# Attention and two MLPs on one core: from the eleventh head on, `v` in two float16 parts and four products a tile instead of three parts and five

## The chip, the cores and the metric

The kernel runs on one core of a Trainium2 chip. The metric is the device time of one execution in microseconds (us), lower is better. Three runs of the kernel before are given, and one further execution that was profiled.

## The reference

```python
scores = scale * np.matmul(q, k.transpose(0, 1, 3, 2))          # 4 batches, 8 heads, 576 positions, 64 wide
decay = cum[:, :, :, None] - cum[:, :, None, :]                 # cum: cumulative sum of log f
scores = np.where(causal, -1000000000.0, scores + decay)
attn = np.exp(scores - np.max(scores, axis=-1, keepdims=True))
attn = attn / (np.sum(attn, axis=-1, keepdims=True) + 1e-09)
x = np.matmul(attn, v)                                          # then (2304, 512)
h = x @ w_in                                                    # 512 -> 2048
x = (np.maximum(h, 0.0) + alpha * np.minimum(h, 0.0)) @ w_out   # 2048 -> 512
out = ((x @ w_a) * (x @ w_b)) @ w_o                             # 512 -> 1536 -> 512
```

All is float32, so the kernel makes its products from parts: a float32 value is a high part plus a remainder, and a product is the sum of the products of the parts that matter.

## The kernel before

**Order of the work.** 32 heads (4 batches of 8) are worked off one after another in `attention()`. Step u runs a list of short operation names that is written out by hand (`_P["even"]`, `_P["odd"]`; `even0` and `odd0` for u below 10): `s0` to `s3` make the scores of head u in four blocks of 128 rows (128, 256, 384 and 512 columns wide) and their softmax numerators, `R` those of the last 64 rows of two heads, `h*` and `l*` split the numerators of head u-1 into two float16 parts and send them through a transposing DMA, `p0` to `p2` multiply the transposed parts of head u-2 with `v` (`pv`), `ri` and `rr` make the reciprocals of the row sums, `T` and `Q` prepare and load `q` and `k`, `V` loads `v` of head u+2, `vs` splits `v` of head u, `X` transposes the result of two heads. Each `M` hands over to the first MLP: from step 10 on `mlp1a` fills the places between with matmuls of the first seven of 16 blocks of `w_in` and `w_out` (names `h`, `y`), for half a batch (288 tokens) at a time. A scheduler then puts the instructions of each engine in an order of its own, within the dependences. After the heads come the rest of the first MLP (`hb`, `ya`) and the second one (`p`, `o`), with no part in the change.

**`v` before.** `load_v` (L344) brings a head into one of five buffers `vs` of three planes, 5 tiles of 128x64 each; the fifth tile has only 64 real rows. `split_v` (L351) makes two remainders on GpSimd, each by a subtraction of 128x320 (L357), so that the high halves of the three planes are three bfloat16 parts. Of the first ten heads six are kept `whole` (heads 0, 1, 4, 5, 8 and 9), with float32 products; all others take this split.

**The products.** `pv` (L511) has 15 tiles a head (10 below the diagonal and on it, 5 for the last rows), and of each five products with 64 columns:

```python
ph, pl = PT[m, grp][:, 2 * b], PT[m, grp][:, 2 * b + 1]
parts = [(ph, 0), (ph, 1), (ph, 2), (pl, 0), (pl, 1)]
for x, (p, i) in enumerate(parts):
    pe.matmul(o, p, high(vs[:, i, t]), start=start and x == 0, stop=stop and x == len(parts) - 1)
```

The numerators carry a factor 2^15 (`PSCALE`); `rinv` (L425) takes it out together with the row sum.

**Queues around it.** All loads and transposes are issued by the sync engine (SP) in order. GpSimd also makes the remainder of the MLP's activations, `g` (L651), which follows `lu` (ScalarE, L648), `lt` (VectorE, L649) and the cast of `g` (ScalarE, L650), and which the `y` matmuls need (L655). At the start GpSimd runs one chain of memsets (`ap_["pool"]`) for the constants of the attention, and behind it those of `rows`, from which the sync engine stores the decay sums.

Of the kernel before, what the change touches and what calls it, by code (L numbers as in the profile page):

```python
# [29 lines left out]
TB = 384  # L30
NQ = 5
PSCALE = 2.0 ** 15
MASK = -8.0e9


REBIAS = 2.0 ** -112
_P = dict(
    even="T h3 h2 h0 h1 s2 vs M Q s0 M l3 l2 s3 ri M p1 s1 l1 l0 M p0 p2 V M W".split(),
    odd="h3 h2 h0 h1 R vs M Q l3 l2 T s2 M h4 s3 ri M p1 s1 l1 l0 M p0 p2 rr s0 V W l4 M X".split(),
    split=0,  # L40
    lag=2,
    eng={'hi': 'act', 'lo': 'act', 'r': 'pool'},
# [7 lines left out]
    es=10,  # L50
    eng0={'e0': 'act', 'e2': 'act', 'e3': 'dve', 'e4': 'act'},
    even0='s3 T p1 s2 vs s0 Q M M M M h3 h2 h0 h1 l1 l2 p0 s1 l0 l3 ri p2 V W M'.split(),
    odd0='h3 h2 h0 h1 R M Q l2 T l3 M p1 s3 h4 s2 l1 l0 M M s1 s0 ri rr p0 vs p2 V W l4 M X'.split(),
)
PSM = _P["psm"]
LAG = _P["lag"]
# [4 lines left out]
def whole(n):  # L61

    return n < NATIVE and n // 2 % 2 == 0
# [26 lines left out]
def decay_attention_then_two_mlps(ctx, tc, q, k, v, f, w_in, w_out, alpha, w_a, w_b, w_o, out):  # L90
# [178 lines left out]
    def attention_setup():  # L269
        a = lpool(right, "att1", 1, "right")  # L270
        ap_["a"] = a
        maskz = a.tile([128, ST + 128 + S - HB], BF16, name="maskz")
        with tc.issue_after(ap_["pool"]):
            pool.memset(maskz, 0.0)
        tri = maskz[:, ST:ST + 128]
        ap_["pool"] = pool.affine_select(
            out=tri, in_=tri, pattern=[[-1, 128]], compare_op=ALU.is_ge, fill=MASK, base=0, channel_multiplier=1,
        ).ins

        def zeros(x):  # L280
            with tc.issue_after(ap_["pool"]):
                ap_["pool"] = pool.memset(x, 0.0).ins
        rest = maskz[:, ST + 128:]
        for j in range(2):
            act.copy(rest[64 * j:64 * j + 64, S - HB - SR:], tri[0:64, 0:SR])
        ap_["mask"] = maskz
        ap_["mask_r"] = rest

        for i in range(2):
            z = ST + SR * (1 - i)  # L290
            scores_set(a, i)
            rq = a.tile([64, SP], F32, tag=f"RQ_{i}", name=f"RQ_{i}")
# [12 lines left out]
        for nm in ("nmr", "smr"):
            ap_[nm] = a.tile([128, 2], F32, tag=nm, name=nm)
        for i in range(5):

            ap_["vs", i] = a.tile([128, 3, NQ, D], F32, tag=f"vs_{i}", name=f"vs_{i}")
            zeros(ap_["vs", i][SR:, :, 4])  # L310

    def load_qk_pool():
        ident = ap_["ident"] = lpool(right, "ident", 1, "right").tile([128, 128], F32, name="ident")
# [31 lines left out]
    def load_v(n):  # L345
# [2 lines left out]
        sp.dma_start(vs[:, 0, 0:4], v[b, h, 0:ST].rearrange("(p t) d -> p t d", p=128))  # L348
        sp.dma_start(vs[0:SR, 0, 4], v[b, h, ST:])

    def split_v(n):  # L351

        if whole(n):
            return
        vs = ap_["vs", n % 5]
        for i in range(2):
            pool.tensor_tensor(vs[:, i + 1], vs[:, i], high(vs[:, i]), op=ALU.subtract)  # L357

# [33 lines left out]

    def scores(n, i):
        w = 128 * (i + 1)
        o = bank(f"sc_{n}_{i}")[:, 0:w]
        products(o, n, 128 * i, 0, w, True, True)
        return o

    def softmax_in(n, i, o):
        s = s_view(n, i)  # L400
        m = ap_["mask"][:, ST - 128 * i:ST - 128 * i + 128 * (i + 1)]
        nm, sm = (ap_[x, n % 2][:, i:i + 1] for x in ("nm", "sm"))
        dve.tensor_tensor_reduce(s, o, m, -0.125, 3.0e38, ALU.add, ALU.min, nm)  # L403
        act.activation(s, s, AF.Exp, bias=nm, scale=-1.0, accum_out=sm)  # L404

    def scores_rest(n):
# [15 lines left out]
        dve.tensor_tensor(nm[:, 0:1], nm[:, 0:1], nm[:, 1:2], op=ALU.min)  # L422
        act.activation(s[:, :S], s[:, :S], AF.Exp, bias=nm[:, 0:1], scale=-1.0, accum_out=sm[:, 0:1])

    def rinv(n, sm, ri):  # L425
        dve.tensor_scalar(sm, sm, 1e-9, 1.0 if whole(n) else PSCALE, op0=ALU.add, op1=ALU.mult)
        dve.reciprocal(ri, sm)

    PT = {}
# [84 lines left out]
    def pv(u, c):  # L514

        g, j = divmod(u, 2)
        vs = ap_["vs", u % 5]
        if u not in ps_x:
            pl = "mm" if u + LAG < max(_P["first"], NATIVE) else "at"
            ps_x[u] = ps[pl].tile([128, 512], F32, tag=pl, name=f"pv_{u}")  # L520
        ps_o = ps_x[u]

        def products(o, m, grp, b, t, start, stop):
            if whole(u):
                pe.matmul(o, P32[m, grp][:, b], vs[:, 0, t], start=start, stop=stop)
                return
            ph, pl = PT[m, grp][:, 2 * b], PT[m, grp][:, 2 * b + 1]
            parts = [(ph, 0), (ph, 1), (ph, 2), (pl, 0), (pl, 1)]
            for x, (p, i) in enumerate(parts):
                pe.matmul(o, p, high(vs[:, i, t]), start=start and x == 0, stop=stop and x == len(parts) - 1)  # L530

        if c < 2:
            for i in (2 * c, 2 * c + 1):
                for t in range(i + 1):
                    products(ps_o[:, D * i:D * i + D], u, GROUP[i], FIRST[i] + t, t, t == 0, t == i)
            return
        for t in range(NQ):
# [48 lines left out]
    def attention():  # L586

        cur = lambda u: 0 <= u < NI
        if LAG == 2:
            load_v(0)  # L590
            load_v(1)
        warm_up(_P.get("wu", [0, 0])[0], "a")
        stack(0)
        warm_up(_P.get("wu", [0, 0])[1], "b")
        load_qk(2)
        if NATIVE > 3:
            load_qk(3)
        yield "W", -1
        for u in range(NI + LAG):
            ap_["u"] = u  # L600
            for op in order(u):
                a, i = op[0], op[-1]
                if op in ("M", "W"):
                    yield op, u
                elif op == "ri":
                    if cur(u - 1):
                        rinv(u - 1, ap_["sm", (u - 1) % 2], ap_["ri", (u - 1) % 2])
                elif op in ("h4", "l4"):
                    m = u if u % 2 else u - 1
                    if cur(m):  # L610
                        (p_hi if a == "h" else p_lo)(m, 4)
                elif a in "hl":
                    if cur(u - 1):
                        (p_hi if a == "h" else p_lo)(u - 1, int(i))
                elif op == "R":
                    if cur(u):
                        softmax_rest(scores_rest(u))
                elif op == "rr":
                    if cur(u):
                        rinv(u, ap_["smr"][:, 0:1], ap_["rir", u // 2 % 2])  # L620
                elif a == "s":
                    if cur(u):
                        softmax_in(u, int(i), scores(u, int(i)))
                elif op == "T":
                    if cur(u + 1):
                        stack(u + 1)
                elif op == "Q":
                    if u > 1 and cur(u + 2):
                        load_qk(u + 2)
                elif op == "V":  # L630
                    if cur(u + 4 - LAG):
                        load_v(u + 4 - LAG)
                elif op == "vs":
                    if cur(u + 2 - LAG):
                        split_v(u + 2 - LAG)
                elif op in ("p0", "p1", "p2"):
                    if cur(u - LAG):
                        pv(u - LAG, int(i))
                elif op == "X":
                    if cur(u - 3):  # L640
                        turn((u - 3) // 2)
# [448 lines left out]
```

## Time and profile before

| | us |
|---|---|
| median of 3 runs | 1050.09 |
| lowest, highest | 1049.08, 1052.24 |
| the profiled execution | 1054.88 |
| its span in the trace | 1053.1 |

The span is the time from the first to the last instruction of the program on the core; the profiled execution has 1.8 us around it. Its own time is 4.79 us above the median. PE is the matmul engine, DVE is VectorE, ACT ScalarE, POOL GpSimd, SP the sync engine, whose issues have the letter q behind the name. An instruction's record reaches from its start to its end; on PE, ACT and DVE the next one can start before that.

### The profile page before, as it was taken

To read this page: it belongs to the slowest core of one execution; us is meant where nothing else is said; L and a number is where in the kernel's file an instruction comes from. 1 tells how busy PE (TensorE), PEld (TensorE's weight loads), DVE (VectorE), ACT (ScalarE), POOL (GpSimd) and SP (SyncE) were. 2 spreads that over 40 slices of the span, in tenths; PEclk is the share of its full clock that TensorE was granted. 3 is DMA by queue.
4 is the path that set the end of the run, shared out by engine and by line. 5 is a ranking of instruction groups with operands and counts; after the bars stand their busy time and mean duration, and the time that the engine had idled before them with its cause. 6 is when DMAs were issued, how large, how long until landed. Compare 5 with 4: busy or idle time off the path is not lost.

```text
span 1053.1 us, 20143 instructions
## 1 busy us (share of the span) xinstructions
PE 1008.3 (96%) x7485; PEld 955.5 (91%) x7485; DVE 704.1 (67%) x1455; ACT 460.2 (44%) x1041; POOL 412.5 (39%) x415
## 2 busy tenths in 40 slices
PE   4788999999999999999999998999999999999998
PEld 3677999999999999999999997999989999899997
DVE  5899878878866275443557749665985558965553
ACT  4767777777865354333344343222442123321110
POOL 4424423324232255333456677322543224531111
PEclk9899999999999999999999999999999999999999
DMA  6995779987994758556668995835338384453623
GB/s 168 211 204 128 192 154 155 218 170 158 225 152 78 250 163 256 195 190 192 228 215 275 345 366 199 319 104 216 110 101 310 114 307 135 124 207 124 250 90 111
DMA packets 191783, 202.90 MB, mean 193 GB/s; under 512 B 99460, under 2 KB 160388, under 8 KB 191684
## 3 DMA queue, kind: packets, MB, share of 16 engines
q1 hardware_dynamic: 191684, 201.60, 65.7%
q8 instruction: 59, 0.97, 0.4%
q14 instruction: 40, 0.33, 0.1%
HBM read 130.07 MB, written 50.17 MB: 171 GB/s over the span
## 4 chain that ended last, share of the span: by engine, by line
PE 75%; DVE 11%; DMA 5%; issue 3%; POOL 3%; ACT 1%; SPq 1%; POOLq 0%; DVEq 0%; ACTq 0%
PE p L654 7%; PE p L656 7%; PE p L655 7%; PE pv L530 5%; PE o L654 4%; PE o L655 4%; PE o L656 4%; PE ya L654 3%; PE ya L655 3%; PE ya L656 3%; PE hb L654 3%; PE hb L656 3%; PE hb L655 3%; PE h L654 2%; PE y L655 2%
## 5 line engine op out<-in xcount | busy, mean ns | idle before, releaser
L654 PE MATMUL p<-yq,w_h 128*128 128x384 f32 x360 | 121.7, 338 | 2.3 <-DVE lu L1033 1.4
L656 PE MATMUL p<-yq,w_h 128*128 128x384 f32 x360 | 121.3, 337 | 0.0
L655 PE MATMUL p<-yq,w_h 128*128 128x384 f32 x360 | 121.1, 336 | 0.0
L654 PE MATMUL o<-w_o,gg 128*128 128x512 f32 x216 | 84.7, 393 | 1.7 <-ACT gg L1014 1.7
L404 ACT ACTIVATE s<-s,nm 128x512 f32<-128x512 f32 (+3 forms) x128 | 71.5, 560 | 32.9 <-DVE nm L403 31.9
L655 PE MATMUL o<-w_o,gg 128*128 128x512 f32 x216 | 84.9, 393 | 0.0
L357 POOL TENSOR_TENSOR vs<-vs 128x320 f32<-128x320 f32 x52 | 43.4, 835 | 101.9 <-DMA vs<-in_v 96.7
L656 PE MATMUL o<-w_o,gg 128*128 128x512 f32 x216 | 83.2, 393 | 0.0
L1015 POOL TENSOR_TENSOR gg<-tc,gg 128x384 fp32r<-128x384 f32 x36 | 36.7, 1018 | 114.1 <-ACT gg L1014 97.0
L651 POOL TENSOR_TENSOR g<-lt,g 128x288 fp32r<-128x288 f32 x56 | 54.0, 972 | 66.8 <-ACT g L650 47.4
L651 POOL TENSOR_TENSOR gb<-lt,gb 128x384 fp32r<-128x384 f32 x54 | 55.8, 1034 | 59.7 <-ACT gb L650 59.6
L654 PEld LDWEIGHTS p<-yq,w_h 128*128 128x128 f32 x360 | 67.6, 188 | 6.9 <-DVE lu L1033 1.7
L1015 POOL TENSOR_TENSOR gg<-td,gg 128x384 fp32r<-128x384 f32 x36 | 38.1, 1057 | 89.3 <-ACT gg L1014 83.6
L1014 ACT CAST gg<-tc 128x384 fp32r<-128x384 f32 x36 | 18.5, 514 | 124.8 <-DVE tc L1013 124.8
L655 PE MATMUL ya<-gb,w_out 128*128 128x384 f32 x216 | 72.8, 337 | 0.0
L656 PE MATMUL ya<-gb,w_out 128*128 128x384 f32 x216 | 72.5, 336 | 0.0
L654 PE MATMUL ya<-gb,w_out 128*128 128x384 f32 x216 | 71.0, 336 | 1.2 <-DVE yl L856 1.2
L649 DVE SCALAR_TENSOR_TENSOR lt<-lu,nal,hb 128x384 f32<-128x384 f32 x54 | 33.0, 611 | 57.9 <-ACT lu L648 57.9
L655 PEld LDWEIGHTS p<-yq,w_h 128*128 128x128 f32 x360 | 67.6, 188 | 3.7
L403 DVE CUSTOM_DVE_ANT_0 s<-sc,maskz 128x512 f32<-128x512 f32 (+3 forms) x128 | 60.4, 483 | 14.0 <-PE sc L391 9.4
L655 PE MATMUL y<-g,w_out 128*128 128x288 f32 x224 | 66.3, 299 | 3.4 <-POOL g L651 3.4
L656 PEld LDWEIGHTS p<-yq,w_h 128*128 128x128 f32 x360 | 67.6, 188 | 0.2
(207 smaller groups left out, 3123.4 us busy)
## 6 DMA issues: line engine op xcount, KB each, us to landing
yq<-yq_d SPq DMA_DIRECT2D x49, 768.0 KB
yq_d<-yhl SPq DMA_DIRECT2D x42, 384.0 KB
yl<-ya_d SPq DMA_DIRECT2D x48, 192.0 KB
po_d<-os SPq DMA_DIRECT2D x36, 256.0 KB
os<-po_d SPq DMA_DIRECT2D x36, 256.0 KB
RK<-in_k SPq DMA_DIRECT2D x44, 144.0 KB
wr_a<-in_moe_w_a SPq DMA_DIRECT2D x12, 512.0 KB
wr_b<-in_moe_w_b SPq DMA_DIRECT2D x12, 512.0 KB
```

The lines of the kernel that those rows point to most:

```text
L357: pool.tensor_tensor(vs[:, i + 1], vs[:, i], high(vs[:, i]), op=ALU.subtract)
L403: dve.tensor_tensor_reduce(s, o, m, -0.125, 3.0e38, ALU.add, ALU.min, nm)
L404: act.activation(s, s, AF.Exp, bias=nm, scale=-1.0, accum_out=sm)
L530: pe.matmul(o, p, high(vs[:, i, t]), start=start and x == 0, stop=stop and x == len(parts) - 1)
L649: dve.scalar_tensor_tensor(t, u, nal[:, fi:fi + 1], hp[:, :n], op0=ALU.mult, op1=ALU.add)
L651: pool.tensor_tensor(gl, t, f32(gh), op=ALU.subtract)
L654: pe.matmul(o, lh, rh, start=start, stop=False)
L655: pe.matmul(o, lh, rl, start=False, stop=False)
L656: pe.matmul(o, ll, rh, start=False, stop=stop)
L1014: ap_["last"] = act.copy(g[:, 0], o).ins
L1015: pool.tensor_tensor(g[:, 1], o, f32(g[:, 0]), op=ALU.subtract)
```

## The change

For heads 10 to 31 (`scaled`), `v` is multiplied by a power of two of its own and split in two float16 parts. `bound_v` (operation `va`) takes the absolute value of a head on ScalarE with its sum by partition; `sum_v` adds these up over the partitions with a matmul of one column against ones, into a spare column of the bank of the 384 wide scores; `scale_v` makes the scale from the exponent bits of that sum, with two steps on VectorE, and two factors for `rinv` on GpSimd, which take the scale out again. `split_v` writes the high part by a scaled cast on ScalarE and the remainder by one operation on VectorE, both into plane 1. The split comes a step later in the list, and the pad rows get a small floor, so that their sum isn't zero. `pv` then has four products a tile.

```diff
-    even="T h3 h2 h0 h1 s2 vs M Q s0 M l3 l2 s3 ri M p1 s1 l1 l0 M p0 p2 V M W".split(),
-    odd="h3 h2 h0 h1 R vs M Q l3 l2 T s2 M h4 s3 ri M p1 s1 l1 l0 M p0 p2 rr s0 V W l4 M X".split(),
+    even="T h3 h2 h0 h1 s2 M Q vs s0 M l3 l2 s3 ri M p1 s1 l1 l0 va M p0 p2 V M W".split(),
+    odd="h3 h2 h0 h1 R vs M Q l3 l2 T s2 M h4 s3 ri M p1 s1 l1 l0 va M p0 p2 rr s0 V W l4 M X".split(),
...
             zeros(ap_["vs", i][SR:, :, 4])
+            with tc.issue_after(ap_["pool"]):
+                ap_["pool"] = pool.memset(ap_["vs", i][SR:, 0, 4], VFLOOR).ins
+        ones = ap_["ones"] = a.tile([128, 128], BF16, name="ones")
+        with tc.issue_after(ap_["pool"]):
+            ap_["pool"] = pool.memset(ones, 1.0).ins
...
+    def bound_v(n):
+        if not scaled(n):
+            return
+        vs = ap_["vs", n % 5]
+        act.activation(vs[:, 2], vs[:, 0], AF.Abs, accum_out=ap_["vm", n % 2][:, 0:1])
+
+    def sum_v(n, o):
+        pe.matmul(o, ap_["ones"], high(ap_["vm", n % 2][:, 0:1]), start=True, stop=True)
+
+    def scale_v(n, o):
+        e, scale, both = (ap_["vm", n % 2][:, i:i + 1] for i in range(1, 4))
+        dve.tensor_scalar(e.bitcast(I32), o.bitcast(I32), 0x7F800000, None, op0=ALU.bitwise_and)
+        dve.tensor_scalar(scale.bitcast(I32), e.bitcast(I32), -1.0, 268.0 * 2 ** 23, op0=ALU.mult, op1=ALU.add)
+        pool.tensor_scalar(both, scale, PSCALE, 1.0, op0=ALU.mult, op1=ALU.mult)
+        a = slice(64 * (n % 2), 64 * (n % 2) + 64)
+        pool.tensor_scalar(ap_["vr", n // 2 % 2][a], scale[a], PSCALE, 1.0, op0=ALU.mult, op1=ALU.mult)
...
         vs = ap_["vs", n % 5]
+        if scaled(n):
+            vh, vl = v_parts(n)
+            scale = ap_["vm", n % 2][:, 2:3]
+            act.activation(vh, vs[:, 0], AF.Copy, scale=scale)
+            dve.scalar_tensor_tensor(vl, vs[:, 0], scale, vh, op0=ALU.mult, op1=ALU.subtract)
+            return
         for i in range(2):
             pool.tensor_tensor(vs[:, i + 1], vs[:, i], high(vs[:, i]), op=ALU.subtract)
...
+        if i == 2 and scaled(n):
+            sum_v(n, t[:, w:w + 1])
         products(o, n, 128 * i, 0, w, True, True)
...
         dve.tensor_tensor_reduce(s, o, m, -0.125, 3.0e38, ALU.add, ALU.min, nm)
+        if i == 2 and scaled(n):
+            scale_v(n, t[:, 128 * (i + 1):128 * (i + 1) + 1])
         act.activation(s, s, AF.Exp, bias=nm, scale=-1.0, accum_out=sm)
...
-            parts = [(ph, 0), (ph, 1), (ph, 2), (pl, 0), (pl, 1)]
-            for x, (p, i) in enumerate(parts):
-                pe.matmul(o, p, high(vs[:, i, t]), start=start and x == 0, stop=stop and x == len(parts) - 1)
+            if scaled(u):
+                vh, vl = (x[:, t] for x in v_parts(u))
+                parts = [(ph, vh), (ph, vl), (pl, vh), (pl, vl)]
+            else:
+                parts = [(p, high(vs[:, i, t])) for p, i in ((ph, 0), (ph, 1), (ph, 2), (pl, 0), (pl, 1))]
+            for x, (p, r) in enumerate(parts):
+                pe.matmul(o, p, r, start=start and x == 0, stop=stop and x == len(parts) - 1)
...
                 elif op == "vs":
-                    if cur(u + 2 - LAG):
-                        split_v(u + 2 - LAG)
+                    for n in (u, u - 1):
+                        if cur(n) and scaled(n) == (n < u):
+                            split_v(n)
```

The scheduler gives the instructions a new order. Three places show it, each around head 24 (line numbers are those of the file that the rows come from).

PE, where step 24 begins: `tx_10` is the transposed result of heads 20 and 21, `sc_24_2` the 384 wide scores. Before, and then with the change:

```order
L558 MATMUL tx_10_0_3931<-ident_89,xn_10_3695 128x128 x2
L558 MATMUL tx_10_1_3936<-ident_89,xn_10_3695 128x128 x2
L560 MATMUL tx_10_1_3936<-fold_172,xr_0_157 128x64
L390 MATMUL sc_24_2_3952<-U1_2_1259,T1_2_1258 128x384
L391 MATMUL sc_24_2_3952<-TU2_2_1260 128x384
```

```order
L614 MATMUL tx_10_0_3845<-ident_89,xn_10_3618 128x128 x2
L614 MATMUL tx_10_1_3850<-ident_89,xn_10_3618 128x128 x2
L616 MATMUL tx_10_1_3850<-fold_172,xr_0_157 128x64
L373 LDWEIGHTS ones_193
L373 MATMUL sc_24_2_3866<-vm_0_195,ones_193 128x1
L433 MATMUL sc_24_2_3866<-U1_2_1274,T1_2_1273 128x384
L434 MATMUL sc_24_2_3866<-TU2_2_1275 128x384
```

The one-column matmul with its weight load stands directly ahead of the scores. In all, the order has 1620 `pv` matmuls in parts instead of 1950, in 77 uninterrupted runs instead of 69.

ACT, at the same place: `p16_23_lo` is the cast of numerators of head 23, `g_1_288` the activation of the second half of batch 1, `s_0` the exponentials of head 24. Before, and then with the change:

```order
L648 ACTIVATE lu_6_3922<-h_1_288_6_3854 128x288
L453 ACTIVATE p16_23_lo_3950<-s_1_165 128x3x128
L562 CAST xh_2_3135<-tx_10_0_3931 128x256
L650 CAST g_1_288_3513<-lt_6_3921 128x288
L562 CAST xh_2_3135<-tx_10_1_3936 128x320
L404 ACTIVATE s_0_152,sm_0_154<-s_0_152,nm_0_153 128x384
L404 ACTIVATE s_0_152,sm_0_154<-s_0_152,nm_0_153 128x128
```

```order
L708 ACTIVATE lu_6_3836<-h_1_288_6_3776 128x288
L453 ACTIVATE s_1_165,sm_1_167<-s_1_165,nm_1_166 128x128
L618 CAST xh_2_3085<-tx_10_0_3845 128x256
L505 ACTIVATE p16_23_lo_3864<-s_1_165 128x3x128
L618 CAST xh_2_3085<-tx_10_1_3850 128x320
L369 ACTIVATE vs_1_181,vm_0_195<-vs_1_181 128x320
L710 CAST g_1_288_3445<-lt_6_3835 128x288
L453 ACTIVATE s_0_152,sm_0_154<-s_0_152,nm_0_153 128x384
L453 ACTIVATE s_0_152,sm_0_154<-s_0_152,nm_0_153 128x128
L396 ACTIVATE vs_4_190<-vs_4_190,vm_0_195 128x5x64
```

The absolute sum (L369) is that of head 26 (buffer 26 mod 5 = 1), and stands ahead of the cast of `g`; the split (L396) is that of head 24 (buffer 4).

SP, around the transposes of head 23: `PT_23` are its transposed numerators, `vs_1` in the order before is the load of head 26. Before, and then with the change:

```order
L512 DMA_TRANSPOSE PT_23_r_3913<-p16_23_r_3776 128x10x128
L348 DMA vs_1_180<-in_v 128x256
L512 DMA_TRANSPOSE PT_23_hi_3983<-p16_23_hi_3948 128x14x128
L349 DMA vs_1_180<-in_v 64x64
L371 DMA TU2_1_161<-cum_d0_72 4x1216
```

```order
L564 DMA_TRANSPOSE PT_23_r_3827<-p16_23_r_3704 128x10x128
L357 DMA vs_3_187<-in_v 128x256
L358 DMA vs_3_187<-in_v 64x64
L414 DMA TU2_1_161<-cum_d0_72 4x1216
L341 DMA RK_0_150<-in_k 64x576
L564 DMA_TRANSPOSE PT_23_hi_3902<-p16_23_hi_3862 128x14x128
```

At the same transposes it is now head 28 (buffer 3) that is loaded.

## Rows read from the trace of the kernel before

**Rows 1.** The page, its first lines: busy time and share of the span.
```profile
span 1053.1 us, 20143 instructions
...
PE 1008.3 (96%) x7485; PEld 955.5 (91%) x7485; DVE 704.1 (67%) x1455; ACT 460.2 (44%) x1041; POOL 412.5 (39%) x415
```

**Rows 2.** Windows, pairs of heads 14 to 29: stretch, length, busy time by engine, granted clock.
```profile
251.64:273.39 21.75, 20.61 (x267) 19.98 (x266) 16.62 (x48) 16.27 (x41) 4.32 (x6) 1.00 0.83 156
...
sum 167.42, PE 164.03 PEld 159.42 DVE 130.13 ACT 125.14 POOL 58.02; mean PE 20.50 PEld 19.93 DVE 16.27 ACT 15.64 POOL 7.25
```

**Rows 3.** Waits, 128 to 348 us, PE's and POOL's: us in total, times, longest.
```profile
PE y L655 <- POOL g L651: 3.4, 3, 1.2
...
POOL vs L357 <- DMA vs<-in_v: 64.4, 16, 8.8
```

**Rows 4.** Windows of line 530 alone (`pv`), 128 to 348 us: PE, then weight loads.
```profile
128.00:348.00 220.00, 58.66 (x1650) 52.31 (x1650) 1.00 0.81 160
```

**Rows 5.** Timeline of PE from 344 us: start, length, line, operation, tiles, count.
```profile
344.05 1.22 PE L530 MATMUL pv<-vs,PT_hi 128*128 128x64 bf16 x35
345.11 0.38 PE L654 MATMUL y<-g,w_out 128*128 128x288 f32 x1
345.33 0.29 PE L655 MATMUL y<-g,w_out 128*128 128x288 f32 x1
345.46 0.30 PE L656 MATMUL y<-g,w_out 128*128 128x288 f32 x1
```

**Rows 6.** Timeline of PE, 248 to 258 us: last `h`, and `y` behind its wait.
```profile
248.94 0.29 PE L656 MATMUL h<-xh,w_in 128*128 128x288 f32 x1
...
256.80 0.40 PE L655 MATMUL y<-g,w_out 128*128 128x288 f32 x1 [1.14 <-POOL g L651]
```

**Rows 7.** Timeline of ACT, 252 to 256 us.
```profile
252.37 0.39 ACT L648 ACTIVATE lu<-h 128x288 f32<-128x288 f32 x1
252.66 0.52 ACT L453 ACTIVATE p_lo<-s 128x384 f16<-128x384 f32 x1
...
253.91 0.43 ACT L650 CAST g<-lt 128x288 fp32r<-128x288 f32 x1 [0.47 <-DVE lt L649]
...
255.18 0.62 ACT L404 ACTIVATE s<-s,nm 128x384 f32<-128x384 f32 x1 [0.52 <-DVE nm L403]
255.70 0.19 ACT L404 ACTIVATION_READ_ACCUMULATOR s<-s,nm 128x1 f32 x1
```

**Rows 8.** Timeline of POOL, 248 to 258 us.
```profile
255.28 0.72 POOL L357 TENSOR_TENSOR vs<-vs 128x320 f32<-128x320 f32 x1 [4.07 <-DMA vs<-in_v]
255.96 0.79 POOL L651 TENSOR_TENSOR g<-lt,g 128x288 fp32r<-128x288 f32 x1
```

**Rows 9.** Timeline of SP, 245 to 312 us: the second part of the load of head 26.
```profile
252.47 1.03 SPq L349 DMA_DIRECT2D vs<-in_v  x1
```

**Rows 10.** Timelines of DVE, from four stretches.
```profile
162.78 0.15 DVE L426 TENSOR_SCALAR smr<-smr 128x1 f32<-128x1 f32 x1
...
163.34 0.81 DVE L506 SCALAR_TENSOR_TENSOR p_r<-sr,p_r 128x640 f16<-128x640 f32 x1
...
173.98 1.44 DVE L506 SCALAR_TENSOR_TENSOR p_hi<-s,p_hi 128x896 f16<-128x896 f32 x1 [1.86 <-ACT p_hi L453]
...
205.77 1.09 DVE L506 SCALAR_TENSOR_TENSOR p_hi<-s,p_hi 128x896 f16<-128x896 f32 x1
...
253.79 0.55 DVE L506 SCALAR_TENSOR_TENSOR p_lo<-s,p_lo 128x384 f16<-128x384 f32 x1
```

**Rows 11.** The chain that ended last, 9 to 14 us: start, length, what.
```profile
10.27 0.09 POOL sr L282
...
10.43 1.34 POOL vs L282 x5
...
13.26 0.33 SPq L230
```

More of the change, by code (lines that the diff above doesn't have):

```diff
@@ L32 @@
 PSCALE = 2.0 ** 15
+VFLOOR = 2.0 ** -90
 MASK = -8.0e9
@@ L52 @@
     even0='s3 T p1 s2 vs s0 Q M M M M h3 h2 h0 h1 l1 l2 p0 s1 l0 l3 ri p2 V W M'.split(),
-    odd0='h3 h2 h0 h1 R M Q l2 T l3 M p1 s3 h4 s2 l1 l0 M M s1 s0 ri rr p0 vs p2 V W l4 M X'.split(),
+    odd0='h3 h2 h0 h1 R M Q l2 T l3 M p1 s3 h4 s2 l1 l0 M M s1 s0 ri rr p0 vs p2 va V W l4 M X'.split(),
 )
@@ L310, in attention_setup @@
             zeros(ap_["vs", i][SR:, :, 4])
+            with tc.issue_after(ap_["pool"]):
[3 more added lines that the diff above has]
+            ap_["pool"] = pool.memset(ones, 1.0).ins
+        for i in range(2):
+            ap_["vm", i] = a.tile([128, 4], F32, tag=f"vm_{i}", name=f"vm_{i}")
+            ap_["vr", i] = a.tile([128, 1], F32, tag=f"vr_{i}", name=f"vr_{i}")
     def load_qk_pool():
@@ L349, in load_v, with scaled, v_parts @@
         sp.dma_start(vs[0:SR, 0, 4], v[b, h, ST:])
+    def scaled(n):
+        return n >= NATIVE
+    def bound_v(n):
[12 more added lines that the diff above has]
+        pool.tensor_scalar(ap_["vr", n // 2 % 2][a], scale[a], PSCALE, 1.0, op0=ALU.mult, op1=ALU.mult)
+    def v_parts(n):
+        t = ap_["vs", n % 5][:, 1].bitcast(F16)
+        return t[..., 0:D], t[..., D:2 * D]
     def split_v(n):
@@ L394, in scores, with softmax_in @@
         w = 128 * (i + 1)
-        o = bank(f"sc_{n}_{i}")[:, 0:w]
+        t = bank(f"sc_{n}_{i}")
+        o = t[:, 0:w]
+        if i == 2 and scaled(n):
+            sum_v(n, t[:, w:w + 1])
         products(o, n, 128 * i, 0, w, True, True)
-        return o
-    def softmax_in(n, i, o):
+        return t
+    def softmax_in(n, i, t):
         s = s_view(n, i)
+        o = t[:, 0:128 * (i + 1)]
         m = ap_["mask"][:, ST - 128 * i:ST - 128 * i + 128 * (i + 1)]
@@ L423, in softmax_rest, with rinv @@
         act.activation(s[:, :S], s[:, :S], AF.Exp, bias=nm[:, 0:1], scale=-1.0, accum_out=sm[:, 0:1])
-    def rinv(n, sm, ri):
-        dve.tensor_scalar(sm, sm, 1e-9, 1.0 if whole(n) else PSCALE, op0=ALU.add, op1=ALU.mult)
+    def rinv(n, sm, ri, vr=None):
+        c = 1.0 if whole(n) else PSCALE
+        if scaled(n):
+            c = ap_["vm", n % 2][:, 3:4] if vr is None else vr
+        dve.tensor_scalar(sm, sm, 1e-9, c, op0=ALU.add, op1=ALU.mult)
         dve.reciprocal(ri, sm)
@@ L619, in attention @@
                     if cur(u):
-                        rinv(u, ap_["smr"][:, 0:1], ap_["rir", u // 2 % 2])
+                        rinv(u, ap_["smr"][:, 0:1], ap_["rir", u // 2 % 2], ap_["vr", u // 2 % 2])
                 elif a == "s":
@@ L632, in attention @@
                         load_v(u + 4 - LAG)
+                elif op == "va":
+                    if cur(u + 1):
+                        bound_v(u + 1)
                 elif op == "vs":
-                    if cur(u + 2 - LAG):
-                        split_v(u + 2 - LAG)
+                    for n in (u, u - 1):
+                        if cur(n) and scaled(n) == (n < u):
+                            split_v(n)
                 elif op in ("p0", "p1", "p2"):
```

## The prediction

> **What bounds the kernel now.** I read the page first, then the windows, then the timelines of the single engines. On the page TensorE (PE) is busy for 1008.3 of 1053.1 us [rows 1]. An average over stages proves nothing, so I cut the stage that the change touches into pairs of heads, from one score matmul of 384 columns to the next but one: eight pairs, heads 14 to 29, 167.42 us, 20.93 us a pair. PE is busy in 164.03 of them at the full granted clock, VectorE (DVE) in 130.13, ScalarE (ACT) in 125.14, GpSimd (POOL) in 58.02 [rows 2]. The 3.4 us that PE lacks lie in three of the pairs, 1.14 of them in the one shown [rows 2]; the other five have no idle PE at all. The waits say what it is: a `y` matmul that waits for POOL's `g`, three times, 3.4 us, and behind it a POOL that waits for the load of `v` [rows 3]. So in this stage a PE instruction removed is time removed, as long as the other engines keep up, and the kernel after it is PE work too. The stretch from 128 to 348 us holds all 22 heads from the eleventh on: 1650 `pv` matmuls, 75 a head [rows 4].
>
> **The change part by part.**
>
> *One product of five goes.* A head has 15 tiles, so 22 heads lose 330 matmuls. Its price is read from start to start, because records overlap: 35 of them start at 344.05 and the next matmul at 345.11 [rows 5], 1.06 us or 30.3 ns each. All of it is on PE's path: 330 x 30.3 ns = **-10.0 us**.
>
> *A one-column matmul by head is added*, ahead of the 384 columns of scores. No row shows one. It costs at least the 30 ns of a small bf16 matmul. It also stands between fp32r matmuls: after the 35 `pv` the next `y` takes 0.22 us from start to start (345.11 to 345.33), where a plain one takes 0.13 (345.33 to 345.46) [rows 5]. That 0.09 us is the price of coming back from 16-bit work. I take 0.12 us, since it is the same change of operand: 22 x 0.12 = **+2.6 us**. The ends are 0.03 (its next load hidden, as after a transpose) and 0.20 us: 0.7 and 4.4 us. The new order also cuts the `pv` runs into 8 more pieces, 8 x 0.09 = **+0.7 us**. The matmul waits for ACT's absolute sum of the same head, but that stands two steps earlier, next to the scores of head n-2, about one pair, 20.9 us, ahead of its own; no stall.
>
> *The split leaves POOL.* Two POOL subtractions a head (0.72 us each) and, above all, their wait for the load of `v` go. Rows 8 show what it did: the cast of `g` ended at 254.34 [rows 7], POOL stood until 255.28 for `v`, split, and began `g` at 255.96 [rows 8]; PE stood 1.14 us and went on at 256.80 [rows 6]. With no split ahead of it `g` would have started at 254.34 and ended near 255.1, while PE wanted it at 256.80 - 1.14 = 255.66. The three stalls go: **-3.4 us**. The wait for the load isn't handed to ACT: a scaled head's raw `v` is dead once it is split, so the loads are issued one to two heads earlier in the queue, while the absolute sum stands about where POOL's split stood. Today's load of that head is issued last at 252.47 and was waited for until 255.28 [rows 8, 9].
>
> *ACT and DVE get it.* ACT: the absolute sum of 128x320 is an activation with an accumulator like the 384 exponential's 0.62 us and 0.19 for the read [rows 7]; a sixth fewer elements make it 0.56, and each of the two starts 0.1 us before the one ahead has ended, so 0.55 us net; the scaled cast, below the 0.52 of 384 elements [rows 7], 0.36 net. Together 0.9 us a head. DVE: the 640 form of its subtraction took 0.81, the 384 form 0.55 [rows 10], so 0.48 us for 320, net 0.40; two scalar steps like the 128x1 of 0.15 [rows 10], net 0.1 each. Together 0.6 us a head. Per pair ACT goes from 15.64 to 17.4 and DVE from 16.27 to 17.5, in a pair that I expect at about 20.2 us. I count both at nothing as throughput: the cover is their idle time, 5.3 and 4.7 us a pair now. As delay they count where PE waits for the last `g` of a half of a batch: `h` ended at 249.23 [rows 6], `lu` began only at 252.37 [rows 7], 3.1 us later, behind other ACT work. Without the split `g` would have been ready 5.9 us after `h`; PE came for it after 6.4. The new order has PE do some 0.3 us more in between (two matmuls of 0.13), but ACT has an absolute sum (0.55) and a cast (0.36) more ahead of the `g` cast, and DVE up to 0.6: 6.8 to 7.4 against 6.7. I take 0.4 us in three of the six halves that lie in the stage, the second ones of each batch: **+1.2 us**. The ends are nothing, and 1.5 us of extra work waited for in all six, 9 us.
>
> The rule that speaks to DVE: at 173.98 a subtraction of 896 elements took 1.44 us while POOL split, and 1.09 at 205.77 [rows 10]. The Trainium skill (SBUF — State Buffer, "SBUF: two separate sides") states that a VectorE operation with two SBUF inputs and a GpSimd operation that reads SBUF exclude each other for a whole instruction. The trace agrees that the two meet, though by 0.35 us and not by a whole instruction. By the rule each new subtraction on DVE could stand behind one of POOL's `g` (0.79 us [rows 8]), 1.6 us a pair: DVE would need 19.1 us, the third rival below would decide at 1.1 us of idle time instead of 2.7, and end near 1082 instead of 1064. On the other side 44 POOL subtractions no longer block DVE. I take the row and leave both out of the sum.
>
> *The prologue.* Six memsets more stand in POOL's chain ahead of `rows`. The chain that ended last runs there: 1.34 us for five memsets of 64x192, then `rows`, and only then the sync queue stores at 13.26 [rows 11]. `sr` (128x64) held it 0.09 us [rows 11]; five of 64x64 at 0.1 and one of 128x128 at 0.15 make **+0.7 us**. PE isn't full there, so this shifts what follows; at best it is absorbed, at worst 0.9.
>
> The sum: -10.0 + 2.6 + 0.7 - 3.4 + 1.2 + 0.7 = **-8.2 us**, against a profiled execution of 1054.88 us. That one is 4.8 us above the median of the three runs, 1050.09; I take the difference over to the median: **1041.9 us**.
>
> **The rivals.**
>
> *A faster pace.* Four products with contiguous float16 instead of every second half of a float32: if 64 columns came to 26.7 ns (64 at 2.4 GHz) instead of 30.3, 1320 remaining matmuls would give 4.8 us more: 1037.1. For it: the clock granted is the full one, so something else takes the 3.6 ns. Against it: nothing in the trace ties that to the stride. Chance 0.10.
>
> *The gain is refilled.* PE reaches the same results sooner, ACT and DVE deliver them later, and `y` waits for `g` in all six halves: with the 9 us instead of 1.2 the sum is -0.4 us, 1049.7. For it: a margin of 0.5 us in the chain of rows 6 to 8. Against it: PE doesn't wait for ACT or DVE itself in these pairs. Chance 0.15.
>
> *DVE becomes the bound* (the slower side). Its idle time, (167.42 - 130.13) / 8 = 4.7 us a pair, is then not slack but waits that it needs for PE and ACT. It decides once more than 20.2 - 17.5 = 2.7 us of it must stay. If all stays, a pair takes 17.5 + 4.7 = 22.2 instead of 20.9, and 11 pairs cost 14 us: 1064. For it: each subtraction on DVE waits for an ACT cast. Against it: five of eight pairs show a PE that never waits, and POOL's 44 subtractions no longer slow DVE. Chance 0.08.
>
> *ACT inherits the wait for `v`.* If the loads came no earlier, the absolute sum would hold ACT as the split held POOL, 64.4 us in 16 waits [rows 3], 4.0 each, against an ACT idle of (20.2 - 17.4) / 2 = 1.4 us a head: up to 2.6 x 22 = 57 us, 1099 if nothing hides. The order of the loads speaks against it. Chance 0.05.
>
> **How the numbers follow.** The forecast has 0.62, with an own range of 1037 to 1047. A measurement of this kernel can tell about 0.3%, 3.2 us, from no change. Faster by more than that: nearly all of the forecast, the faster pace, a sixth of the refilled case: 0.75. Within it: the rest of the refilled case and the weak end of the forecast, 0.14. Slower: the last two but for their mild forms, 0.11. The range leaves out the two slow cases (0.13) and little else: from 1035 (no new stall, no prologue, part of the faster pace) to 1050.
>
> **What would show it.** Right: 1320 `pv` matmuls of 22 heads at 30 ns from start to start; the one-column matmul and the next fp32r matmul together 0.12 us longer; pairs of 20.2 us; POOL without a wait for `v`; PE's waits for `g` near 1 us in all; DVE near 87% and ACT near 86% of a pair. Wrong: pairs of 20.9 us or more; PE waiting in the score matmuls, at the one-column matmul, or at `y` for `g` by more than 4 us; ACT waiting for the load; a first score matmul more than 1 us later than now.

## The result, and the profile after

| | before | after |
|---|---|---|
| median, us | 1051.16 (4 runs) | 1039.18 (4 runs) |
| lowest, highest | 1049.08, 1052.47 | 1038.62, 1040.8 |
| profiled execution | 1054.88 | 1038.62 |
| stage: scores of head 10 to the last `pv`, profiled | 246.1 | 233.8 |

The ratio is 0.989, with a 95% interval of 0.9868 to 0.9912: **12.0 us faster** (9.3 to 13.9). The forecast of 1041.9 is 2.7 us too high, inside its range; of the change it had 8.2 us, of which 12.0 came. The stage's row was worked out from the two timelines, from the start of its first score matmul to that of its last `pv`:

```profile
101.49 0.42 PE L390 MATMUL sc<-U,T 128*128 128x384 f32 x1
...
346.85 0.91 PE L530 MATMUL pv<-vs,PT_r 128*128 128x64 bf16 x25
```

```profile
98.00 0.42 PE L433 MATMUL sc<-U,T 128*128 128x384 f32 x1
...
331.21 0.75 PE L586 MATMUL pv<-vs,PT_r 128*128 128x64 f16 x20
```

Its difference, 12.3 us, is as large as the whole gain. That is one execution each: two more of the order before, e13_before_again and e3_late_split below, took 244.4 and 243.8 us for the stage, so the difference is 10.0 to 12.3.

The page of the kernel after, where before stood 1053.1 us and 1008.3 us of PE [rows 1]:

```profile
span 1036.8 us, 19681 instructions
...
PE 996.1 (96%) x7177; PEld 941.9 (91%) x7177; DVE 712.5 (69%) x1521; ACT 477.1 (46%) x1107; POOL 394.3 (38%) x421
```

The windows of the kernel after, cut by the same rule as [rows 2] (stretch, length, busy time of PE, weight loads, DVE, ACT, POOL, then the granted clock):

```profile
277.62:301.75 24.13, 22.28 (x256) 21.37 (x254) 19.49 (x58) 17.33 (x47) 5.19 (x8) 1.00 0.92 164
sum 160.28, PE 158.43 PEld 152.69 DVE 139.16 ACT 137.98 POOL 44.75; mean PE 19.80 PEld 19.09 DVE 17.40 ACT 17.25 POOL 5.59
```

Eight pairs take 160.28 us where they took 167.42: 20.03 us each. PE is busy in all but 1.85 us, and these lie in the last pair alone. DVE has 87% of a pair, ACT 86%.

The waits of the kernel after (us in total, times, longest), PE's from 90 to 350 us and POOL's from 128 to 332 us:

```profile
PE pv L586 <- DMA PT_r<-p_r: 1.8, 1, 1.8
PE h L714 <- DVE xl L619: 1.1, 1, 1.1
PE tp L515 <- DVE vm L378: 0.4, 1, 0.4
...
POOL vm L380 <- DVE vm L379: 26.1, 13, 8.7
```

Compared with [rows 3], `y` no longer waits for `g` and POOL no longer for the load of `v`. POOL stands instead for its two small scale steps (26.1 us), and no matmul of the stage waits for POOL. New is one wait of PE for the transposed numerators of the last rows, `PT_r`.

The timeline of PE after, three places (start, length, line, operation, tiles, count):

```profile
239.94 0.33 PE L616 MATMUL tx<-fold,xr 128*128 128x64 f32 x2
240.11 0.17 PE L373 MATMUL sc<-vm,ones 128*128 128x1 bf16 x1
240.14 0.42 PE L433 MATMUL sc<-U,T 128*128 128x384 f32 x1
240.40 0.34 PE L434 MATMUL sc<-TU 68*128 68x384 f32 x1
...
249.59 0.18 PE L373 MATMUL sc<-vm,ones 128*128 128x1 bf16 x1
249.63 0.42 PE L433 MATMUL sc<-U,T 128*128 128x384 f32 x1
249.89 0.33 PE L434 MATMUL sc<-TU 68*128 68x384 f32 x1
...
283.66 0.64 PE L586 MATMUL pv<-vs,PT_hi 128*128 128x64 f16 x16
284.13 0.36 PE L433 MATMUL sc<-U,T 128*128 128x256 f32 x1
...
284.73 0.52 PE L586 MATMUL pv<-vs,PT_lo 128*128 128x64 f16 x12
287.10 0.26 PE L586 MATMUL pv<-vs,PT_r 128*128 128x64 f16 x3 [1.85 <-DMA PT_r<-p_r]
```

And of PE before, the 384 columns at an even head and at an odd one:

```profile
251.50 0.33 PE L560 MATMUL tx<-fold,xr 128*128 128x64 f32 x2
251.64 0.42 PE L390 MATMUL sc<-U,T 128*128 128x384 f32 x1
251.90 0.34 PE L391 MATMUL sc<-TU 68*128 68x384 f32 x1
...
262.59 0.30 PE L656 MATMUL y<-g,w_out 128*128 128x288 f32 x1
262.72 0.34 PE L390 MATMUL sc<-U,T 128*128 128x384 f32 x1
262.90 0.34 PE L391 MATMUL sc<-TU 68*128 68x384 f32 x1
```

Sixteen `pv` in 0.47 us make 29.4 ns each. The one-column matmul takes 0.03 to 0.04 us from start to start. Behind it the first matmul of 384 columns takes 0.26 us. At an even head it did so before as well (251.64 to 251.90), since it follows the matmul of the last rows; only at an odd head is it new (0.18 before).

### The profile page after: what moved, and what is told of

Read it like the earlier page. It is cut to its first block, busy times and chain, and to the rows that moved or that the text cites. A ratio compares the mean times of both kernels' runs of the same rounds, so it can differ in the third digit from the quotient of the medians.

```text
span 1036.8 us, 19681 instructions
## 1 busy us (share of the span) xinstructions
PE 996.1 (96%) x7177; PEld 941.9 (91%) x7177; DVE 712.5 (69%) x1521; ACT 477.1 (46%) x1107; POOL 394.3 (38%) x421
## 4 chain that ended last, share of the span: by engine, by line
PE 77%; DVE 9%; DMA 5%; issue 3%; ACT 2%; POOL 2%; SPq 1%; ACTq 0%; DVEq 0%; POOLq 0%
PE p L714 7%; PE p L716 7%; PE p L715 7%; PE o L716 4%; PE o L714 4%; PE o L715 4%; PE pv L586 4%; PE hb L714 3%; PE ya L714 3%; PE ya L715 3%; PE hb L716 3%; PE hb L715 3%; PE ya L716 3%; PE y L714 2%; PE y L715 2%
## 5 line engine op out<-in xcount | busy, mean ns | idle before, releaser
L711 POOL TENSOR_TENSOR g<-lt,g 128x288 fp32r<-128x288 f32 x56 | 57.3, 1031 | 103.0 <-ACT g L710 102.1
L714 PE MATMUL h<-xh,w_in 128*128 128x288 f32 x224 | 66.5, 301 | 1.1 <-DVE xl L619 1.1
L715 PE MATMUL h<-xl,w_in 128*128 128x288 f32 x224 | 66.1, 296 | 0.0
```

The lines of the kernel that those rows point to most:

```text
L711: pool.tensor_tensor(gl, t, f32(gh), op=ALU.subtract)
L714: pe.matmul(o, lh, rh, start=start, stop=False)
L715: pe.matmul(o, lh, rl, start=False, stop=False)
```

## The experiments

"Stage" is the stretch of the table above in each kernel's one profiled execution: 246.1 us before, 233.8 after. "Before" is the median of its own runs beside each experiment, 1051.3 to 1053.2.

### Half of the change alone: fewer products, or the new split

**e1_four_old** is the kernel before without the fifth product (the low numerators by the second part of `v`).

```diff
             parts = [(ph, 0), (ph, 1), (ph, 2), (pl, 0), (pl, 1)]
+            if u >= NATIVE:
+                parts = parts[:4]
```

> The kernel before, but heads 10 to 31 leave out the fifth product (low part of the numerators times the second part of v), so it computes less; split, queues and waits stay as they were. If a product costs its 30.3 ns on PE's path: 330 x 30.3 ns = 10.0 us less than before, ratio 0.9905, and the three waits of y for POOL's g stay near 3.4 us. If those waits take up what PE saves, because PE is there sooner and the load of v is not: 3 to 5 us less, ratio 0.995 to 0.997, with 8 us or more of waits for g.

Measured: 1047.64 us against 1051.29, ratio 0.9959 (0.9935 to 0.9983); stage 241.8. Of some 10 us only 4 arrive. Its waits (PE, then POOL):

```profile
PE y L657 <- POOL g L653: 6.2, 2, 3.9
...
POOL vs L357 <- DMA vs<-in_v: 58.7, 13, 8.0
```

Its timelines at the longer of the two, of POOL and of PE:

```profile
286.37 0.72 POOL L357 TENSOR_TENSOR vs<-vs 128x320 f32<-128x320 f32 x1 [8.01 <-DMA vs<-in_v]
287.05 0.79 POOL L653 TENSOR_TENSOR g<-lt,g 128x288 fp32r<-128x288 f32 x1
```

```profile
283.72 0.29 PE L656 MATMUL y<-g,w_out 128*128 128x288 f32 x1
287.89 0.61 PE L657 MATMUL y<-g,w_out 128*128 128x288 f32 x1 [3.88 <-POOL g L653]
288.30 0.45 PE L658 MATMUL y<-g,w_out 128*128 128x288 f32 x1
...
289.74 0.45 PE L657 MATMUL y<-g,w_out 128*128 128x288 f32 x1
289.98 0.45 PE L658 MATMUL y<-g,w_out 128*128 128x288 f32 x1
```

POOL stood 8.01 us for the load of `v`, split, and began `g`; PE stood 3.88 us for that `g`. So the wait of [rows 3] grew from 3.4 to 6.2 us. It costs more than its length: behind it the matmuls of 288 columns come 0.24 us apart (289.74 to 289.98), not 0.13, because the granted clock is lower:

```profile
274.00:283.00 9.00, 9.00 (x114) 8.71 (x113) 7.87 (x18) 7.07 (x19) 2.34 (x3) 1.00 1.15 264
283.00:292.00 9.00, 5.12 (x26) 4.88 (x25) 4.00 (x9) 3.69 (x8) 3.66 (x5) 0.69 0.91 184
```

Over the stage the matmuls of 288 columns, from start to start and less the pauses behind them, sum to 147.4 us where they had 144.9. The account: 10.2 us of `pv` (50.2 to 40.1, summed in the same way), less 2.8 of longer waits and 2.5 of slower matmuls, leaves 4.9; the stage shows 4.3.

**e2_five_new** is the kernel after with the last product made twice, so five again with the new split.

```diff
-                parts = [(ph, vh), (ph, vl), (pl, vh), (pl, vl)]
+                parts = [(ph, vh), (ph, vl), (pl, vh), (pl, vl), (pl, vl)]
```

> The changed kernel, with the fourth product of a tile made twice (so its output is off in the lowest bits): five products again, all else new. If the product count carries its 10 us of the 12.0: 2 us faster than before, ratio 0.998. If the gain comes from the split that left POOL and from the earlier loads: 8 to 12 us faster, ratio 0.989 to 0.992. If the new instructions cost more than they give without the fifth product: slower than before.

Measured: 1047.3 us, ratio 0.9959 (0.9943 to 0.9975); stage 239.9. PE idles nowhere in the stage (0.06 us). From start to start the `pv` matmuls take 48.7 us, and 39.4 in the kernel after (41.2 less its pause of 1.85 at `PT_r`). So the product alone is worth 9.3 us, and the kernel after gives 1.85 of them back at `PT_r`: some 7.4 are left. The medians, 1047.3 and 1039.18, are 8.1 us apart. The stages differ by 6.1 us, since in the kernel after the matmuls of 288 columns also sum to 1.0 us more (145.5 against 144.6) and another wait takes 0.4.

### What holds POOL: its work or the load

**e3_late_split** puts the old split later in the written list.

```diff
-                    if cur(u + 2 - LAG):
-                        split_v(u + 2 - LAG)
+                    for n in (u, u - 1):
+                        if cur(n) and (n >= NATIVE) == (n < u):
+                            split_v(n)
```

> The kernel before with the split of heads 10 to 31 one step later in the list, still on POOL, three parts and five products. If POOL's wait for the load of v is what holds g: the three waits of y go, 3.4 us less, ratio 0.9968. If POOL then meets the transposes or g in another place: no change, ratio 0.999 to 1.002, with a new wait named at y or pv.

Measured: 1052.21 us, ratio 1.0002 (0.9985 to 1.002). The experiment tells nothing about POOL: the scheduler put the split back between the same `g`, and PE's waits for `g` were 2.7 us in three. PE, POOL, ACT, DVE and the sync queue run the same sequence as in the kernel before, so its trace is a further look at that kernel (stage 243.8). What it does tell is that this shift in the list moved no instruction.

**e6_five_early** keeps the old split and all five products, but frees the raw plane early: a third POOL operation copies the high halves away, so the next load can be issued sooner.

```diff
             pool.tensor_tensor(vs[:, i + 1], vs[:, i], high(vs[:, i]), op=ALU.subtract)
+        if n >= NATIVE:
+            pool.tensor_copy(vs[:, 1].bitcast(BF16)[..., 0::2], high(vs[:, 0]))
...
+                r = high(vs[:, i, t])
+                if i == 0 and u >= NATIVE:
+                    r = vs[:, 1, t].bitcast(BF16)[..., 0::2]
...
```

> The kernel before, five products and the split on POOL, but for the heads from the eleventh on a third POOL operation copies the high halves into the unused low halves of plane 1, so that the raw plane is free after the split: the sync queue then issues these loads one to two heads earlier, as the changed kernel does. Theory (it is the wait for the load, not the work, by which POOL's split holds g): POOL waits for in_v hardly at all in spite of 22 x 0.7 us more work, PE's waits for g fall from some 3 us to under 1, and the time from 1051 to about 1048. Rival (POOL's own work ahead of g is what costs): a longer split holds g longer, PE's waits for g grow above 3 us, 1051 to 1055.

**e7_four_early** is the same without the fifth product, so e1_four_old with early loads.

```diff
-            parts = [(ph, 0), (ph, 1), (ph, 2), (pl, 0), (pl, 1)]
+            parts = [(ph, 0), (ph, 1), (ph, 2), (pl, 0), (pl, 1)][:4 if u >= NATIVE else 5]
```

> The same early loads with the split on POOL, and the fifth product left out for the heads from the eleventh on (as in e1_four_old, which gave only 4 us). Theory (the 10 us of the product are lost where g stands behind a POOL that waits for the load): with the wait gone, the 10.0 us come in full and the stalls go, 1051 - 10 - 3 = about 1038. Rival (fewer products gain only with the new split, because POOL's work itself or something else limits): about 1047 as in e1_four_old.

Measured: e6_five_early 1051.34 us, ratio 0.9994 (0.9982 to 1.0006), stage 243.4; e7_four_early **1040.76 us**, ratio 0.9886 (0.9868 to 0.9905), stage 233.7, as short as that of the kernel after. The waits of e7_four_early (PE's two, and POOL's):

```profile
PE tp L465 <- DVE nm L405: 2.0, 2, 1.6
PE h L659 <- DVE xl L568: 1.1, 1, 1.1
...
POOL vs L357 <- PE pv L535: 47.4, 11, 7.3
...
POOL vs L357 <- DMA vs<-in_v: 1.7, 1, 1.7
```

With the products cut, early loads turn 4 us into 11, although POOL does more work; PE's sequence is the same as in e1_four_old, while ACT's and DVE's differ in places. So POOL's work isn't what cost; when its split is released is. But half of what I expected fell: POOL waits nearly as long as before, now for a `pv` matmul, the last reader of the planes that the split writes. That release comes early enough for `g`; the load's, which is issued only after the same buffer is free, did not. And early loads alone gave nothing clear of noise (0.7 us between the medians), not 3: one wait for `g` of 2.4 us stayed in e6_five_early, and the granted clock of the stretch from 132 to 138 us around it and behind it was 0.72.

### The scale and its matmul

**e4_const** leaves out the absolute sum, the one-column matmul and the scale steps, and uses a constant 16.

```diff
-        act.activation(vs[:, 2], vs[:, 0], AF.Abs, accum_out=ap_["vm", n % 2][:, 0:1])
+        return
...
-            scale = ap_["vm", n % 2][:, 2:3]
+            scale = 16.0
...
-            sum_v(n, t[:, w:w + 1])
```

> The changed kernel without the absolute sum, the one-column matmul and the scale steps; v is multiplied by the constant 16. If the one-column matmul costs PE 0.12 us a head with its changes of operand: 2.6 us less than the changed kernel, ratio to before 0.9865. If only its own 0.03 us count: 0.7 us less, ratio 0.988. If ACT's or DVE's extra work was what held PE: 4 us less or more, ratio below 0.985.

**e9_sum_pv** leaves nothing out; it puts the one-column matmul at the end of a `pv` run, where the change of operand is paid anyway.

```diff
-        if i == 2 and scaled(n):
-            sum_v(n, t[:, w:w + 1])
...
                         pv(u - LAG, int(i))
+                    if op == "p1" and cur(u) and scaled(u):
+                        o = ps_x[u - LAG][:, 5 * D:5 * D + 1]
+                        sum_v(u, o)
+                        scale_v(u, o)
```

> The changed kernel with the one-column matmul at the end of a run of pv matmuls (in a spare column of their bank) instead of ahead of the 384 columns of scores; nothing left out. Theory (its price is the change of operand, 0.09 us each, not its own 30 ns): 22 x 0.09 = 2.0 us less than the changed kernel, about 1037, and the score matmul of 384 columns behind starts 0.17 us after the one ahead again. Rival (the scale comes later, the split and with it pv wait for it): no gain, PE waiting at pv for DVE or ACT, 1039 or more.

Measured: e4_const 1037.03 us, ratio 0.9869 (0.9836 to 0.9903), stage 230.3; e9_sum_pv 1039.51 us, ratio 0.9878 (0.9855 to 0.9902), stage 231.9. Both intervals cover the kernel after. The timelines tell the price better: summed over the stage, the first matmuls of the 384 columns take from start to start

| us | even heads | odd heads |
|---|---|---|
| before | 2.85 | 1.93 |
| after | 2.86 | 2.89 |
| e4_const | 2.86 | 1.95 |
| e9_sum_pv | 2.85 | 2.02 |

plus 0.76 us in the kernel after for the one-column matmuls themselves. So the price is 0.76 + 0.96 = 1.7 us, and e9_sum_pv saves some 1.0 of it, too little for these medians. In e9_sum_pv PE doesn't wait at `PT_r`, but 1.9 us for DVE at the transposes of the result (`tx`).

### Can one more product go

**e8_three** drops one product more, that of the two low parts.

```diff
-                parts = [(ph, vh), (ph, vl), (pl, vh), (pl, vl)]
+                parts = [(ph, vh), (ph, vl), (pl, vh)]
```

> The changed kernel with three products a tile: the product of the two low parts is left out. Theory (PE is still what bounds the stage): 330 x 30 ns = 9.9 us less again, 1039 - 10 = about 1029, pairs of 19.1 us. Rival (ACT and DVE at 17.3 and 17.4 us of a pair need their remaining idle time as waits, so the stage stops getting shorter): pairs stay at 19.7 us or more, 1035 to 1039, with PE waiting for DVE, ACT or POOL.

Measured: **1043.04 us**, ratio 0.9914 (0.99 to 0.9928); stage 234.5. None of the forecast 10 us came. By the medians it is 3.9 us slower than four products; all four of its times (1042.82 to 1043.4) lie above those of the kernel after (up to 1040.8), though the two ratios' intervals overlap. Its waits, and the timeline of PE at the longer one:

```profile
PE pv L586 <- DMA PT_r<-p_r: 7.3, 2, 4.8
```

```profile
283.29 0.32 PE L586 MATMUL pv<-vs,PT_lo 128*128 128x64 f16 x5
288.43 0.61 PE L586 MATMUL pv<-vs,PT_r 128*128 128x64 f16 x8 [4.82 <-DMA PT_r<-p_r]
```

Its windows there, DVE at 5.94 of 6 us ahead of the pause, and a lower clock in it and behind it:

```profile
277.00:283.00 6.00, 5.48 (x61) 5.06 (x59) 5.94 (x17) 4.56 (x14) 2.08 (x2) 1.00 1.00 169
283.00:289.00 6.00, 1.18 (x21) 1.02 (x17) 2.28 (x9) 5.51 (x16) 2.68 (x5) 0.67 1.15 162
289.00:295.00 6.00, 6.00 (x39) 5.74 (x39) 2.60 (x10) 1.14 (x2) 0.00 (x0) 0.76 0.29 67
```

**e10_three_sum** joins e8_three and e9_sum_pv; **e11_three_pool** is e8_three with the loads of `v` on POOL's queue; **e12_three_both** has both.

```diff
-        sp.dma_start(vs[:, 0, 0:4], v[b, h, 0:ST].rearrange("(p t) d -> p t d", p=128))
+        (pool if scaled(n) else sp).dma_start(vs[:, 0, 0:4], v[b, h, 0:ST].rearrange("(p t) d -> p t d", p=128))
...
```

> e8_three and e9_sum_pv together: three products a tile, and the one-column matmul at the end of a run of pv matmuls. The sync queue then issues the transpose of the last rows' numerators (PT_r) of head 27 ahead of that of the next head, where e8_three had it behind it. Theory (e8_three lost its 10 us to PE's 7.3 us of waits for PT_r, and to the lower clock after them): without these waits the product comes in full, 1039.5 - 9.9 = about 1030. Rival (any shorter stage runs into ACT, DVE or the queues somewhere): new waits of 5 us or more elsewhere, 1037 to 1043.

> e8_three with the two loads of v of the heads from the eleventh on issued by POOL and not by the sync engine. Theory (PT_r is late because the sync queue, with 16 to 23 us of issues in a pair of 17 to 28 us, works it off behind other issues): 22 x about 1.8 us of issues leave the sync queue, PE's waits for PT_r shrink from 7.3 to under 3 us, and the time falls from 1043 to about 1033. Rival (PT_r is late since its numerators are late, or its transfer slow): the same 7 us of waits, 1043; POOL's g may be held by the issues on top.

> Three products, the one-column matmul behind a run of pv, and the loads of v on POOL's queue. If both remedies hold, 1028 to 1030 and no PE wait above 2 us in the stage; if POOL's issues hold up g, PE waits at y for g and the time is above that of e10_three_sum.

Measured: 1039.14 us (ratio 0.9873, 0.9851 to 0.9896), 1038.95 (0.9877, 0.9852 to 0.9902) and 1040.36 (0.9888, 0.9869 to 0.9908): none beats four products. In e10_three_sum the wait for `PT_r` is gone and one for another transpose stands in its place; the row below it is the window in which the first half of that wait falls, with ACT busy in 8.00 of 8 us and DVE in 7.89:

```profile
PE pv L582 <- DMA PT_lo<-p_lo: 6.9, 2, 3.7
```

```profile
185.00:193.00 8.00, 4.80 (x82) 4.17 (x81) 7.89 (x24) 8.00 (x24) 1.90 (x3) 0.87 1.08 351
```

In e11_three_pool the sync queue's relief does shrink the wait, from 7.3 to 0.7 us, and the time by 4 us; the other 6 us don't come, and a wait for DVE's scale step is new:

```profile
PE pv L586 <- DVE vm L378: 2.0, 1, 2.0
...
PE pv L586 <- DMA PT_r<-p_r: 0.7, 1, 0.7
```

In e12_three_both the longest wait in the stage is 3.6 us, for `PT_lo` again, and none is at `y` for `g`. The three stages took 231.1, 233.7 and 229.9 us in the one execution of each that was profiled (that of e11_three_pool, 1043.51 us, is the slowest of its six): up to 3.9 us less than with four products, and the medians show none of it.

So with three products the rival held: a further product removed from PE no longer shortens the stage by its price. Transposes on the sync queue, DVE and ACT each hold PE in turn; which of them would have to be relieved first isn't shown.

### The kernel before once more

> The kernel before once more, unchanged, for a second profiled execution. The first one stood 4.8 us above the median, with 3.4 us of waits for g in the stage. Theory (the waits for g belong to the program): the same two or three waits of y for g, 2.5 to 3.5 us in all, POOL waiting some 64 us for in_v, and the stage from head 10 to the last pv at 242 to 246 us. Rival (they belong to that one execution, and so do most of the 4.8 us): waits for g below 1 us, and the stage 3 us shorter or more.

Measured: the profiled execution took 1048.52 us, the first one 1054.88, with the same program. Its waits for `g`:

```profile
PE y L655 <- POOL g L651: 2.6, 4, 0.9
```

The stage took 244.4 us (246.1). The scores of head 10 began at 96.9 us, in the first execution at 101.5: 4.6 of the 6.4 us lie ahead of the stage. So the waits for `g` belong to the program (2.6 and 3.4 us here, 2.7 in e3_late_split), and most of the rest to one execution.

## Why the prediction was right, step by step

- **The bound.** PE bounded the stage before and bounds it after: 158.43 of 160.28 us busy. Pairs of 20.03 us came where I forecast 20.2, DVE 17.40 (17.5), ACT 17.25 (17.4).
- **The product, -10.0.** Held in size: 9.3 us of `pv` between e2_five_new and after, 10.2 between before and e1_four_old. The rival of a faster pace fell as to its size: inside the runs a `pv` matmul takes 29.7 ns on average in the kernel after and 29.5 in e2_five_new, against 30.4 before, where the rival had 26.7. That is worth some 1 us, not 4.8; whether the contiguous operand or its type does it, no run separates.
- **The one-column matmul, +2.6.** Mis-sized: 1.7. I charged the change of operand at all 22 heads, but at the 11 even ones it was paid before, behind the matmul of the last rows. A row that shows this stood in the trace before (251.64 to 251.90).
- **Eight more `pv` pieces, +0.7.** Not separable: the matmuls of 288 columns, less their pauses, sum to 144.9 us before and 145.5 after, but e2_five_new, with the same split, has 144.6.
- **The split leaves POOL, -3.4.** The three waits went, as the theory had it; the second look at the kernel before gives their size as 2.6. That the earlier load matters, which I named only as the reason why ACT would not inherit the wait, is the larger part of the matter: without it the product is worth 4 us (e1_four_old), with it 11 (e7_four_early). The sum treated the two terms as independent. They are not: that the -10.0 could be added in full held because the same change moved the loads, and the working didn't ask what the old split would do to a PE that comes for `g` earlier. In that the forecast was lucky.
- **New waits for `g`, +1.2.** Failed as to the place and the cause: none came. 1.85 us came at `PT_r` instead, and there it was not work on ACT or DVE that came last. DVE had the numerators ready at 276.71; the sync queue, which issued one transfer after the other from 270 us on, came to their transpose at 281.87, and PE went on at 287.10. No run of four products takes other issues off that queue; with three, e11_three_pool does, and the waits for `PT_r` fall from 7.3 to 0.7 us.

```profile
275.29 1.42 DVE L558 SCALAR_TENSOR_TENSOR p_r<-sr,p_r 128x640 f16<-128x640 f32 x1 [0.29 <-POOL p_r L507]
275.99 1.39 POOL L711 TENSOR_TENSOR g<-lt,g 128x288 fp32r<-128x288 f32 x1
281.87 2.04 SPq L564 DMA_TRANSPOSE PT_r<-p_r  x1
```

- **The prologue, +0.7.** Not seen: PE's first matmul starts at 13.26 us, before at 13.25. By the scores of head 10 the executions differ by up to 5 us with or without it, so a loss below that can't be excluded there.
- **The stricter rule on DVE and POOL** (the Trainium skill, SBUF — State Buffer, "SBUF: two separate sides"). The prediction misread its row: the trace agrees with the rule's whole instruction. At 173.98 only 0.49 us of POOL's subtraction were left, since it had begun at 173.75:

```profile
173.75 0.72 POOL L357 TENSOR_TENSOR vs<-vs 128x320 f32<-128x320 f32 x1
```

In the rows above, DVE's 640 wide subtraction, 0.81 to 0.83 us in eleven of its 13 places in that trace, takes 1.42 beside a `g` that had begun at 275.23. The next `g` begins at 275.99 and takes 1.39 instead of some 0.8, ending 0.67 behind the subtraction. In the traces before and after, 20 times a `g` begins while a subtraction of numerators or of `v` runs on DVE, and each time it ends 0.66 to 0.67 us after the last of these. As a price for the new work the rule still overstated: DVE needs 17.40 us a pair, not 19.1, since of the 22 new subtractions 17 meet no POOL operation of any length, four started first and held `g`, and one was held (0.73 us instead of 0.55). POOL's `g` grew from 972 to 1031 ns on average, 3.3 us over 56, and no matmul of the stage waited for it.
- **The other rivals.** The refilled gain (1049.7) and DVE as the bound (1064) didn't come; but e8_three comes near the second one product further on: DVE is busy in 5.94 of 6 us ahead of the long pause, though what PE then waits for is a transpose. ACT didn't inherit the wait for `v`: it has none.

Read by measured terms, from the first execution of before and from e13_before_again: the `pv` in parts, product and pace together, fell by 10.8 and 11.0 us (50.2 and 50.4 to 39.4), PE's waits in the stage by 3.0 and 2.1 (5.2 and 4.4 to 2.3); the one column took 1.7 and the matmuls of 288 columns 0.6 to 0.7 more. That makes 11.5 and 10.7 us, where the stage gained 12.3 and 10.6; the medians differ by 12.0 (9.3 to 13.9). The forecast of 8.2 lies below that interval: it charged the one column 0.9 too much and a prologue of 0.7 that doesn't show, had the pace at nothing, and leaves out a wait of PE that has nothing to do with `g` (`tp` for DVE: 1.8 and 0.9 us in the two executions before, 0.4 after). No kernel here is measurably faster than the one after; e4_const is 2 us below it, inside both intervals, and its fixed scale is not the same computation.

## What to carry to other kernels

A product removed from a full matmul engine is worth its time only if what it waits for can come earlier by as much: look up for each operand which release sets its time, and whether that release itself moves. Buffers that are free earlier can be worth more than the work that frees them: e7_four_early gains 7 us on e1_four_old with one POOL operation more a head. A mean busy share can hide a stretch that is full: DVE and ACT stood at 87% and 86% over a pair with four products, and DVE was busy in 5.94 of the 6 us ahead of the long pause with three; the next saving on PE was lost there.

## What the runs showed of the hardware

A pause of PE can cost more than its length. In the kernel after, the 1.85 us pause left the granted clock at 1.00. In e1_four_old the window around the 3.88 us pause shows 0.69, and the matmuls of 288 columns behind it ran 0.24 us apart, against 0.13 ahead of it, which is the lower of the two levels, 1.2 against 2.4 GHz. In e8_three it was 0.67 around 4.82 us and 0.76 in the 6 us behind. There the matmuls of 288 columns, less their pauses, sum to 2.5 us more than in the kernel after (148.0 against 145.5), for 7.3 us of waits. Shorter pauses did the same: 2.33 us at 204 us in e1_four_old (0.88 from 200 to 206 and 0.84 from 206 to 212), 2.36 in e6_five_early (0.72 from 132 to 138) and 2.48 in e8_three (0.81 from 203 to 212), while one of 2.03 us in e11_three_pool left it at 1.00 (207 to 217). I had costed every wait at its length alone.
